# Two heads share one tile and one store in the last ten pairs of a decode block's backward pass

## The chip, the cores and the metric

The kernel runs on one core of one Trainium2 chip. The time is device microseconds of one execution of the whole program. The core has engines that run their own instruction streams in order: TensorE (PE, with its weight loads as PEld), VectorE (DVE), ScalarE (ACT), GpSimd (POOL) and SyncE (SP, which here only issues DMAs). DMAs run on 16 DMA engines that all queues share: q1 carries what SP issues, q0 what POOL issues, q10 what ScalarE issues.

## The reference, cut to what matters

The program is the forward pass of a transformer block for one new token, and the gradients of all its inputs. Two batches, 32 heads, a cache of 4096 rows of 128 numbers per head, everything in bfloat16:

```python
q = (x @ wq).reshape(B, Sq, Hq, Dh)                      # transposed to b h q d
scores = einsum("bhqd,bhkd->bhqk", q, k) * (Dh ** -0.5)
p = softmax(scores, axis=-1)
o = einsum("bhqk,bhkd->bhqd", p, v)                      # then @ wo
h  = x + attention(layernorm(x))
h2 = h + relu(layernorm(h) @ w1) @ w2
# outputs: h2 and the gradients of x, k_cache, v_cache, wq, wo, w1, w2
```

For one head with probabilities p (4096 numbers), query q, and go, the gradient of that head's attention output, the gradients of the caches are outer products: gV[s, :] = p[s] * go, and gK[s, :] = p[s] * (V[s, :] . go - o . go) * q * scale. Each is 1 MiB, and 64 heads (two batches) have both: 128 MiB are written for them alone, and 64 MiB of K and 64 MiB of V are read, most of V twice.

## The kernel before, in words

A head's 4096 rows lie on 128 partitions, 32 rows each (`NSC` = 32), so that a tile is [128, 32, 128] bfloat16: 8 KiB per partition, 1 MiB in all, one DMA (`load_tile`, L461). A first pass (`p1_iter`, L468) computes scores, softmax and the sums that the forward output needs, and keeps the probabilities in `P_bf`. Between the passes `middle_gen` (L746) and `go_group` (L683) make the MLP and the vectors `goc`, `gom`, `qsc`, `rt` and `negdot` of each head. A second pass takes the 64 heads in the order `turns`; some V tiles were kept, the other 52 are loaded again as `Wt`.

The second pass of one head is `p2_iter` (L869) and, one turn later, `p2_tail` (L848):

- PE spreads go and the scaled q of the head over 128 partitions into a PSUM bank `dp_ps` (L878); ScalarE copies that to `rb`, scaled by `rt` (L883); POOL makes `pp`, the probabilities, each written twice (L885).
- In four groups of eight row blocks, `pair_transpose` (L434) transposes V on PE (L442, two banks in turn), ScalarE copies the result to `t_sb` (L447), and `pair_matvec` (L450) multiplies it by go into `dp_ps` (L455).
- VectorE makes gV in two halves (`outer_half`, L841, at L843), and POOL stores it (L911). In the last three heads ScalarE makes four of the 32 row blocks of gV (L910, with `pf` from POOL).
- In the tail VectorE makes `gsp` = (dp + negdot) * p (L854), then gK in two halves (L843), and POOL stores it (L862).

The turn of head j runs the tail of head j - 1 between its own steps. All instructions are written out in this order by the program; nothing is rescheduled later. Between two steps of a turn, background generators put in one piece each: `fin_gen` (weight gradients, stored from `ot` on ScalarE's queue, L981), the rest of `middle_gen`, and `gx_gen`, whose 40 products over wq on VectorE (L669, `gxp`) fall into the last part of the run.

Large tiles come from one set of 8 KiB homes, which are lent under tags: `ld` for loads, `g` for gV and gK, `f` for `ot`, `q` for wq and w2 tiles. `share` says how many homes each tag may own at a stage. When the last go is known (j = 44), the memory of wo becomes free and gives six more homes: one `ld`, two `g`, three `q`; from then on `g` may own seven, `ld` six. A tile is free again when its store has landed. `pump` (L1149) issues the queue of loads in order as long as an `ld` home is free.

```python
for tag in ("ld", "g", "g", "q", "q", "q"):
    more_home(tag, big3)
...
share(ld=5 + held + more, g=5 + 2 * more, f=3, q=2 + 3 * more)
```

Of the kernel before, what the change touches and what calls it, by code (L numbers as in the profile page):

```python
# [7 lines left out]
FP32 = mybir.dt.float32  # L8
BF16 = mybir.dt.bfloat16
# [6 lines left out]
def kernel(  # L16
# [20 lines left out]
    nc = tc.nc  # L37
# [41 lines left out]


    NBIG = 13
    homes = {"ld": list(range(NBIG)), "g": [], "f": [], "q": []}
    free = {tag: len(v) for tag, v in homes.items()}
    owned = dict(free)
    wanted = {}
# [11 lines left out]

    def goes_to(tag):

        if owned[tag] > wanted.get(tag, len(pools)):  # L100
            for other in homes:
                if owned[other] < wanted.get(other, 0):
                    return other
        return tag
# [329 lines left out]
    def pair_transpose(nat, g, dve=False, busy=0):  # L434
# [12 lines left out]
            nc.scalar.copy(out=t_sb[:], in_=t_ps[:])  # L447
        return t_sb

    def pair_matvec(dst, t_sb, g, vecs):  # L450
        v = t_sb[:].bitcast(BF16).rearrange("p j (k two) -> p j k two", two=2)
        for j in range(GT // 2):
            sc = g * GT + 2 * j
            for par in range(2):
                nc.tensor.matmul(dst[:, sc:sc + 2], lhsT=v[:, j, :, par], rhs=vecs[:, par, :],  # L455
                                 start=(par == 0), stop=(par == 1))
# [4 lines left out]
    def load_tile(what, i, tag):  # L461
        t = take(tag, [128, NSC, 128], what + "t")
        nc.sync.dma_start(out=t[:], in_=natural(A_k_cache if what == "K" else A_v_cache,
                                                *(turns if what == "W" else pairs)[i]))
        (S2 if what == "W" else S1).setdefault(i, {})[what] = t
        (S2 if what == "W" else S1)[i][what + "g"] = tag

    def p1_iter(i, dve_group, busy):  # L468

# [378 lines left out]
    def p2_tail(j):  # L848

        p = S2[j]  # L850
        bp, hp = turns[j]
        pair_matvec(p["dp"], p.pop("T3"), 3, gom[:, bp, hp, :, :])
        gsp = small.tile([128, NSC, 2], BF16, tag="gsp", bufs=2, name="gsp")
        nc.vector.scalar_tensor_tensor(  # L854
            out=gsp[:], in0=p["dp"][:, :, None].to_broadcast([128, NSC, 2]), scalar=negdot[:, hp, bp:bp + 1],
            in1=P_bf[:, p_slot[(bp, hp)], :, None].to_broadcast([128, NSC, 2]), op0=ALU.add, op1=ALU.mult)
        yield
        gK = take("g", [128, NSC, 128], "gK")
        outer_half(gK, p["rb"][:, 128:256], gsp, 0)
        yield  # L860
        outer_half(gK, p["rb"][:, 128:256], gsp, 1)
        nc.gpsimd.dma_start(out=natural(out_2, bp, hp), in_=gK[:])  # L862
        give(gK)
        del S2[j]
        yield

    NSB = 8

    def p2_iter(j, nsb):  # L869

        tail = p2_tail(j - 1) if j - 1 in S2 and "T3" in S2[j - 1] else iter(())
# [12 lines left out]
        pp = small.tile([128, NSC, 2], BF16, tag="pp", bufs=2, name="pp")  # L884
        nc.gpsimd.tensor_copy(out=pp[:], in_=P_bf[:, p_slot[(b, h)], :, None].to_broadcast([128, NSC, 2]))  # L885
# [12 lines left out]
        c["T2"] = pair_transpose(c["W"], 2)  # L898
        pair_matvec(c["dp"], c.pop("T1"), 1, go)
        yield  # L900
        c["T3"] = pair_transpose(c["W"], 3)
        give(c["W"], "g" if j < H and j != 1 and owned["g"] < 3 else None)
        pair_matvec(c["dp"], c.pop("T2"), 2, go)
        gV = take("g", [128, NSC, 128], "gV")
        outer_half(gV, c["rb"][:, 0:128], c["pp"], 0)
        yield
        outer_half(gV, c["rb"][:, 0:128], c["pp"], 1, HALF - nsb)
        if nsb:
            for k in range(nsb):
                nc.scalar.activation(out=gV[:, NSC - nsb + k, :], in_=rb[:, 0:128], func=ACT.Copy, scale=pf[:, k:k + 1])  # L910
        nc.gpsimd.dma_start(out=natural(out_3, b, h), in_=gV[:])  # L911
        give(gV)
        yield
# [209 lines left out]
    while i <= NP1 + 1 or j <= NP1:  # L1123
        ii = i if i <= NP1 + 1 else None
        jj = j if i >= NP1 or (i >= P2_AT and (i - P2_AT) % 2 == 0) else None
        plan.append((ii, jj))
        i += 1
        if jj is not None:
            j += 1


    queue = []
# [3 lines left out]
    for n, (ii, jj) in enumerate(plan):  # L1136
        if ii is not None:
            if ii < NP1:
                queue.append(("K", ii))
        if ii is not None and ii >= 2:  # L1140
            queue.append(("V", ii - 2))
        ahead = plan[n + 1][1] if n + 1 < len(plan) and ii is not None else jj
        if ahead is not None and ahead < NP1 and turns[ahead] not in kept and ("W", ahead) not in queue:
            queue.append(("W", ahead))
        if ii in W_AT:
            queue.append(("w", W_AT.index(ii)))
        if ii in W2_AT:
            queue.append(("w2", W2_AT.index(ii)))
    def pump():  # L1149
        while queue:  # L1150
            what, k = queue[0]
            if what == "w":
                load_weights(k)
            else:
                tag = "ld"
                if free["ld"] < 1:
                    return
                if what == "w2":
# [24 lines left out]
    for n, (i, j) in enumerate(plan):  # L1183
# [7 lines left out]
        if all_go and not late[0]:  # L1191
            wop.release()
            big3 = tc.alloc_tile_pool(name="big3", bufs=1, side="right")
            for tag in ("ld", "g", "g", "q", "q", "q"):
                more_home(tag, big3)
        late[0] = all_go
        more = int(late[0])
        if fin is not None and not bg2 and not bg3:
            share(ld=8 + 3 * more, g=7 + 3 * more)
        elif fin is not None and j >= H:  # L1200
            held = sum(bh in kept for bh in turns[j + 1:])
            share(ld=5 + held + more, g=5 + 2 * more, f=3, q=2 + 3 * more)
        while g2 is not None:
            p2_step()
        open_tail = [k for k in S2 if "T3" in S2[k]]
        if j is not None:
            if j < NP1:
                bg_until(("go", *turns[j]))
            nsb = 0 if i is not None else NSB if j < H and fin is None else NSB // 2 if j >= NP1 - 3 else 0
            g2 = p2_iter(j, nsb) if j < NP1 else p2_tail(NP1 - 1)  # L1210
        elif open_tail:
            g2 = p2_tail(open_tail[0])
        if i is None and ("w1", 1) in done and fin is None:
# [17 lines left out]
        if i is None:  # L1231
            spread[0] = 2
            at_k[0] = 1
            k = 0
            while g2 is not None:
                p2_step()
                pump()
                slot[0] = int(k in ((1, 3, 5) if j <= H else (1, 4)))
# [69 lines left out]
```

## Time and profile before

| what | value |
|---|---|
| median of 3 runs | 894.2 us (891.58 to 896.1) |
| the profiled execution | 892.4 us |
| its span | 890.6 us |
| PE / VectorE / ScalarE / POOL busy | 83% / 77% / 53% / 23% |
| moved by DMA | 361.84 MB, mean 406 GB/s |
| q1 / q0 / q10, share of 16 engines | 58.1% / 36.2% / 4.1% |
| gV and gK stores | 64 each, 1024 KB, 15.1 and 15.4 us to landing |
| Wt loads | 52, 1024 KB, 11.8 us to landing |
| first gV store of the last 20 heads | issued at 705.65 us |

The busy shares are means over stages with different limits, so the stage of a change has to be looked at by itself. The page's slices give the tenths in which each engine is busy and the GB/s that the DMA engines moved; a DMA share of 1 means that all 16 engines had a packet all the time. Waits name what came last before an engine went on. "Packet records" are the DMA engines' own list of packets in the trace, with queue, size, start and duration of each; they do not say which of the 16 engines carried one.

### The profile page before, as it was taken

How to read it: one execution, taken by the hardware profiler on the slowest of the kernel's cores; microseconds unless marked ns; L12 is line 12 of the kernel's file. 1: busy time of each engine (PE TensorE's matmuls, PEld its weight loads, DVE VectorE, ACT ScalarE, POOL GpSimd, SP SyncE). 2: the span in 40 equal slices, each digit the busy share in tenths (PEclk: the TensorE clock that was granted, in tenths of full speed). 3: DMA queues.
4: the chain of work that ended last, by engine and by line, in shares of the span. 5: the costliest groups of instructions: out<-in, count | busy, mean ns of one | idle time of the engine just before them, and what ended most of it. 6: DMA issues, size and time to landing. Idle time of an engine off the chain costs nothing. (4 is left out here: it accounts for less than half of the span.)

```text
span 890.6 us, 24645 instructions
## 1 busy us (share of the span) xinstructions
PE 740.5 (83%) x10145; PEld 622.4 (70%) x10145; DVE 687.8 (77%) x1283; ACT 469.7 (53%) x1184; POOL 204.3 (23%) x342
## 2 busy tenths in 40 slices
PE   4999899999999998888888767885888888658871
PEld 4887788888887887777777656764666665536561
DVE  2665779876789897796796888786988467899992
ACT  1344334443455665454547766554567766437751
POOL 1344434342310000000023321121323011111141
PEclk9999989999999999997995555555557765555555
DMA  9999999999889999999999999999999999999995
GB/s 377 419 411 404 409 407 419 410 415 408 350 325 369 422 422 424 422 421 424 422 390 423 420 419 420 419 416 416 391 404 413 424 425 425 424 426 424 423 421 245
DMA packets 56304, 361.84 MB, mean 406 GB/s; under 512 B 5696, under 2 KB 11904, under 8 KB 15488
## 3 DMA queue, kind: packets, MB, share of 16 engines
q1 hardware_dynamic: 34536, 211.13, 58.1%
q0 software_dynamic: 18432, 134.23, 36.2%
q10 hardware_dynamic: 3224, 14.92, 4.1%
q8 instruction: 80, 1.31, 0.6%
q14 instruction: 32, 0.26, 0.1%
HBM read 211.11 MB, written 149.13 MB: 404 GB/s over the span
## 5 line engine op out<-in xcount | busy, mean ns | idle before, releaser
L447 ACT COPY t_sb<-t_ps 128x512 f32<-128x512 f32 x479 | 273.1, 587 | 186.3 <-PE t_ps L442 181.7
L455 PEld LDWEIGHTS <-t_sb 128*128 128x128 bf16 x4096 | 169.9, 103 | 83.7 <-ACT t_sb L447 42.3
L442 PE MATMUL t_ps<-ident_f,Wt 128*128 128x128 f32 x832 | 201.0, 393 | 0.4 <-ACT t_sb L447 0.4
L483 DVE TENSOR_TENSOR pk<-Kt,ep 128x2048 bf16<-128x2048 bf16 x128 | 156.2, 1221 | 44.7 <-ACT ep L534 24.9
L476 PE MATMUL m_ps<-pk,Vt 128*128 128x129 bf16 x2048 | 176.1, 223 | 13.3 <-DMA Vt<-in_A_v_cache_dram 12.6
L843 DVE TENSOR_TENSOR gK<-rb,gsp 128x2048 bf16<-128x2048 bf16 x128 | 153.8, 1226 | 28.0 <-DMA out_dram<-gV 26.2
L843 DVE TENSOR_TENSOR gV<-rb,pp 128x2048 bf16<-128x2048 bf16 (+2 forms) x128 | 147.1, 1172 | 30.8 <-DMA out_dram<-gK 24.0
L442 PEld LDWEIGHTS t_ps<-ident_f,Wt 128*128 128x128 f32 x832 | 140.4, 205 | 31.9 <-issue 25.0
L442 PE MATMUL t_ps<-ident_f,Kt 128*128 128x128 f32 x1024 | 154.7, 287 | 4.6 <-DMA Kt<-in_A_k_cache_dram 4.5
L476 PEld LDWEIGHTS <-Vt 128*128 128x128 bf16 x2048 | 131.0, 99 | 16.9 <-DMA Vt<-in_A_v_cache_dram 14.9
L442 PEld LDWEIGHTS t_ps<-ident_f,Kt 128*128 128x128 f32 x1024 | 117.0, 148 | 6.1 <-issue 3.4
L493 POOL COPY pk<-ep 128x16 bf16<-128x16 bf16 x80 | 83.1, 1041 | 151.3 <-ACT ep L534 112.7
L455 PE MATMUL dp_ps<-gom,t_sb 128*128 128x2 bf16 x2048 | 96.0, 168 | 23.3 <-ACT t_sb L447 22.9
L911 POOL DMA_DIRECT2D out_dram<-gV x64 | 34.3, 536 | 307.8 <-DVE nb L526 114.3
L455 PE MATMUL s_ps<-gom,t_sb 128*128 128x2 bf16 x2048 | 80.2, 164 | 1.2 <-DVE t_sb L445 1.2
L862 POOL DMA_DIRECT2D out_dram<-gK x64 | 34.1, 533 | 202.0 <-DVE gK L843 156.8
L593 ACT CAST MT<-m_ps 128x128 bf16<-128x128 f32 x64 | 17.1, 266 | 116.3 <-PE m_ps L476 116.3
L978 ACT CAST ot<-o_ps 128x512 bf16<-128x512 f32 (+3 forms) x152 | 67.0, 498 | 9.7 <-DMA out_dram<-ot 8.5
L883 ACT ACTIVATE rb<-dp_ps,rt 128x256 bf16<-128x256 f32 x64 | 30.2, 472 | 46.5 <-PE dp_ps L878 44.8
L669 DVE CUSTOM_DVE_ANT_0 rows<-wo_t,rows 128x640 bf16<-128x640 bf16 x64 | 52.3, 817 | 0.4 <-ACT rows L647 0.2
L669 DVE CUSTOM_DVE_ANT_0 rows<-wqs,gqr 128x1024 bf16<-128x1024 bf16 x40 | 48.8, 1219 | 0.2
L669 DVE CUSTOM_DVE_ANT_0 rows<-w_t,rows 128x640 bf16<-128x640 bf16 (+2 forms) x58 | 45.8, 790 | 1.2 <-ACT rows L647 0.5
(194 smaller groups left out, 720.4 us busy)
## 6 DMA issues: line engine op xcount, KB each, us to landing
Kt<-in_A_k_cache_dram SPq DMA_DIRECT2D x64, 1024.0 KB, 16.4
Vt<-in_A_v_cache_dram SPq DMA_DIRECT2D x64, 1024.0 KB, 16.6
out_dram<-gV POOLq DMA_DIRECT2D x64, 1024.0 KB, 15.1
out_dram<-gK POOLq DMA_DIRECT2D x64, 1024.0 KB, 15.4
Wt<-in_A_v_cache_dram SPq DMA_DIRECT2D x52, 1024.0 KB, 11.8
out_dram<-ot ACTq DMA_DIRECT2D x6, 960.0 KB, 12.4
wq_t<-in_A_wq_dram SPq DMA_DIRECT2D x5, 1024.0 KB, 11.0
wqs<-in_A_wq_dram SPq DMA_DIRECT2D x5, 1024.0 KB, 16.1
```

Source lines behind the costliest of these rows:

```text
L442: nc.tensor.transpose(t_ps[:, j, :], natf[:, 2 * cc:2 * cc + 2, :].rearrange("p c k -> p (c k)"), ident_f[:])
L447: nc.scalar.copy(out=t_sb[:], in_=t_ps[:])
L455: nc.tensor.matmul(dst[:, sc:sc + 2], lhsT=v[:, j, :, par], rhs=vecs[:, par, :], start=(par == 0), stop=(par == 1))
L476: nc.tensor.matmul(r["m"][:, 0:129], lhsT=r["V"][:, sc, :], rhs=r["pk"][sc // HALF][:, sc % HALF, 0:129], start=(sc == 0), stop=(sc == NSC ...
L483: nc.vector.tensor_tensor(out=p["pk"][k][:, :, 0:128].rearrange("p s (a two) -> p s a two", two=2), in0=p["K"][:, sl, :].rearrange("p s (a ...
L493: nc.gpsimd.tensor_copy(out=col, in_=e)
L669: nc.vector.tensor_tensor_reduce(out=junk[0:kc, 0:width], in0=in0, in1=in1, scale=1.0, scalar=0.0, op0=ALU.mult, op1=ALU.add, accum_out=acc)
L843: nc.vector.tensor_tensor(out=pairs_view(dst[:, sl, :]), in0=row.rearrange("p (a two) -> p a two", two=2)[:, None, :, :].to_broadcast([128 ...
L862: nc.gpsimd.dma_start(out=natural(out_2, bp, hp), in_=gK[:])
L883: nc.scalar.activation(out=rb[:], in_=bank[:, 128:384], func=ACT.Copy, scale=rt[:, b, h:h + 1])
L911: nc.gpsimd.dma_start(out=natural(out_3, b, h), in_=gV[:])
L978: nc.scalar.copy(out=ot[0:P, k, n0:n0 + nn], in_=o_ps[0:P, 0:nn])
```

## The change

The last 20 heads of the second pass (j from 44 on, `PAIRS_AT`) are made two by two. Partitions 0 to 63 hold the first head and 64 to 127 the second, so that a partition has 64 rows of one head instead of 32. Two loads of 1 MiB bring V of the pair: each takes 32 of the 64 rows of every partition. `rb`, `pp`, `gsp` are built by halves of the partitions: PE spreads the vectors over 64 partitions each, the probabilities are brought to their partitions by matmuls with `sel` and copied from PSUM by ScalarE, POOL copies the two values of `rt` to one column, and `gsp` is two VectorE instructions of 64 partitions. There are eight groups of transposes and matvecs per pair, whose matvecs serve both heads. gV and gK of a pair are tiles of 16 KiB per partition, made in four `outer_half` instructions each and stored by one DMA of 2 MiB, 16 KiB contiguous per partition; the last pair's two tiles are stored in two halves each. The memory of wo becomes three homes of 16 KiB (`gp`) instead of six of 8 KiB, and the other homes that held gV and gK go to the loads. ScalarE no longer makes part of gV in the last heads.

```diff
-    homes = {"ld": list(range(NBIG)), "g": [], "f": [], "q": []}
+    homes = {"ld": list(range(NBIG)), "g": [], "f": [], "q": [], "gp": []}
...
+    def both_matvec(dst, t_sb, g, vecs):
+        v = t_sb[:].bitcast(BF16).rearrange("p j (k two) -> p j k two", two=2)
+        for j in range(GT // 2):
+            sc = g * GT + 2 * j
+            for par in range(2):
+                nc.tensor.matmul(dst[:, :, sc:sc + 2], lhsT=v[:, j, :, par], rhs=vecs[:, :, par, :],
+                                 start=(par == 0), stop=(par == 1))
...
+    def pair_natural(cache, b, h):
+        return cache[b, h:h + 2].rearrange("h (p sc) d -> (h p) sc d", sc=2 * NSC)
+
+    def load_half(i, k, tag):
+        t = take(tag, [128, NSC, 128], "Wt")
+        nc.sync.dma_start(out=t[:], in_=pair_natural(A_v_cache, *turns[i])[:, k * NSC:(k + 1) * NSC, :])
+        S2.setdefault(i, {})[f"W{k}"] = t
...
+    def by_half(dst, src, h):
+        for k in range(2):
+            rows = slice(64 * k, 64 * k + 64)
+            nc.gpsimd.tensor_copy(out=dst[rows], in_=src[rows, h + k:h + k + 1])
+
+    def both_tail(j):
+        p = S2[j]
+        bp, hp = turns[j]
+        both_matvec(p["dp"], p.pop("T7"), 7, gom[:, bp, hp:hp + 2, :, :])
+        gsp = spare(2)
+        for k in range(2):
+            rows = slice(64 * k, 64 * k + 64)
+            nc.vector.scalar_tensor_tensor(
+                out=gsp[rows], in0=p["dp"][rows, k, :, None].to_broadcast([64, 2 * NSC, 2]),
+                scalar=negdot[rows, hp + k, bp:bp + 1], in1=p["pp"][rows], op0=ALU.add, op1=ALU.mult)
+        yield
+        gK = take("gp", [128, 2 * NSC, 128], "gK")
+        dst = pair_natural(out_2, bp, hp)
+        for k in range(4):
+            outer_half(gK, p["rb"][:, 128:256], gsp, k)
...
+            nc.gpsimd.dma_start(out=dst, in_=gK[:])
...
+    def both_iter(j):
...
+        for k, col in enumerate((goc, qsc)):
+            for q in range(2):
+                nc.tensor.matmul(bank[64 * q:64 * q + 64, 128 + k * 128:256 + k * 128],
+                                 lhsT=col[:, h + q, b:b + 1].to_broadcast([128, 64]), rhs=ident_bf[:],
+                                 start=True, stop=True)
+        pps = bank[:, 384:512].rearrange("p (k q s) -> p k q s", k=2, q=2)
+        for q in range(2):
+            for k in range(2):
+                nc.tensor.matmul(pps[:, k, q, :], lhsT=sel[:, q, :, :].rearrange("p c k -> p (c k)"),
+                                 rhs=P_bf[:, p_slot[(b, h + k)], :], start=True, stop=True)
...
+        by_half(rts, rt[:, b, :], h)
+        rb = mats.tile([128, 256], BF16, tag="rb", bufs=3, name="rb")
+        nc.scalar.activation(out=rb[:], in_=bank[:, 128:384], func=ACT.Copy, scale=rts)
+        pp = spare(j // 2 % 2)
+        for k in range(2):
+            rows = slice(64 * k, 64 * k + 64)
+            nc.scalar.copy(out=pp[rows].rearrange("p (q s) t -> p q s t", q=2),
+                           in_=pps[rows, k, :, :, None].to_broadcast([64, 2, NSC, 2]))
...
+        for g in range(1, 8):
+            W = c[f"W{g // 4}"]
+            c[f"T{g}"] = pair_transpose(W, g % 4)
...
+            both_matvec(c["dp"], c.pop(f"T{g - 1}"), g - 1, go)
+            if g >= 4:
+                if gV is None:
+                    gV = take("gp", [128, 2 * NSC, 128], "gV")
+                outer_half(gV, c["rb"][:, 0:128], c["pp"], g - 4)
...
+            nc.gpsimd.dma_start(out=pair_natural(out_3, b, h), in_=gV[:])
...
+    PAIRS_AT = 2 * H - 2 * (H - 2 * KEPT[1]) // 2
...
-            for tag in ("ld", "g", "g", "q", "q", "q"):
-                more_home(tag, big3)
+            for _ in range(3):
+                more_home("gp", big3)
...
-            share(ld=8 + 3 * more, g=7 + 3 * more)
+            share(ld=16)
...
-            share(ld=5 + held + more, g=5 + 2 * more, f=3, q=2 + 3 * more)
+            share(ld=5 + held + 3 * more, g=5 if not more else int(j == PAIRS_AT), f=3, q=2 + 3 * more)
...
-            g2 = p2_iter(j, nsb) if j < NP1 else p2_tail(NP1 - 1)
+            g2 = both_iter(j) if PAIRS_AT <= j < NP1 else p2_iter(j, nsb) if j < NP1 else both_tail(NP1 - 2)
```

More of the change, by code (lines that the diff above doesn't have):

```diff
@@ L98, in goes_to @@
     def goes_to(tag):
-        if owned[tag] > wanted.get(tag, len(pools)):
+        if tag != "gp" and owned[tag] > wanted.get(tag, len(pools)):
             for other in homes:
@@ L865, in p2_tail, with tail_of, spare @@
         yield
+    def tail_of(j):
+        if j - 1 in S2 and "T3" in S2[j - 1]:
+            return p2_tail(j - 1)
+        if j - 2 in S2 and "T7" in S2[j - 2]:
+            return both_tail(j - 2)
+        return iter(())
+    def spare(k):
+        return P_bf[:, 2 + 4 * k:6 + 4 * k, :].rearrange("p a (s t) -> p (a s) t", t=2)
+    def by_half(dst, src, h):
+        for k in range(2):
+            rows = slice(64 * k, 64 * k + 64)
+            nc.gpsimd.tensor_copy(out=dst[rows], in_=src[rows, h + k:h + k + 1])
@@ new lines, in both_tail @@
+    def both_tail(j):
[13 more added lines that the diff above has]
+            outer_half(gK, p["rb"][:, 128:256], gsp, k)
+            if j == NP1 - 2 and k == 1:
+                nc.gpsimd.dma_start(out=dst[:, 0:NSC, :], in_=gK[:, 0:NSC, :])
+            if k < 3:
+                yield
+        if j == NP1 - 2:
+            nc.gpsimd.dma_start(out=dst[:, NSC:2 * NSC, :], in_=gK[:, NSC:2 * NSC, :])
+        else:
+            nc.gpsimd.dma_start(out=dst, in_=gK[:])
+        give(gK)
+        del S2[j]
+        yield
@@ new lines, in both_iter @@
+    def both_iter(j):
+        tail = tail_of(j)
+        c = S2[j]
+        next(tail, None)
+        b, h = turns[j]
+        go = gom[:, b, h:h + 2, :, :]
+        bank = pst([128, 512], FP32, "sps", "dp_ps")
+        for k, col in enumerate((goc, qsc)):
[8 more added lines that the diff above has]
+                                 rhs=P_bf[:, p_slot[(b, h + k)], :], start=True, stop=True)
+        c["dp"] = bank[:, 0:4 * NSC].rearrange("p (k s) -> p k s", k=2)
+        rts = Uc[:, 0, j // 2 % 2:j // 2 % 2 + 1]
+        by_half(rts, rt[:, b, :], h)
[6 more added lines that the diff above has]
+                           in_=pps[rows, k, :, :, None].to_broadcast([64, 2, NSC, 2]))
+        c.update(rb=rb, pp=pp)
+        c["T0"] = pair_transpose(c["W0"], 0)
+        next(tail, None)
+        yield
+        for _ in tail:
+            yield
+        gV = None
+        for g in range(1, 8):
+            W = c[f"W{g // 4}"]
+            c[f"T{g}"] = pair_transpose(W, g % 4)
+            if g % 4 == 3:
+                give(W)
+            both_matvec(c["dp"], c.pop(f"T{g - 1}"), g - 1, go)
[3 more added lines that the diff above has]
+                outer_half(gV, c["rb"][:, 0:128], c["pp"], g - 4)
+                if j == NP1 - 2 and g == 5:
+                    nc.gpsimd.dma_start(out=pair_natural(out_3, b, h)[:, 0:NSC, :], in_=gV[:, 0:NSC, :])
+            yield
+        if j == NP1 - 2:
+            nc.gpsimd.dma_start(out=pair_natural(out_3, b, h)[:, NSC:2 * NSC, :], in_=gV[:, NSC:2 * NSC, :])
+        else:
+            nc.gpsimd.dma_start(out=pair_natural(out_3, b, h), in_=gV[:])
+        give(gV)
+        yield
+        yield
@@ L867 @@
     NSB = 8
+    PAIRS_AT = 2 * H - 2 * (H - 2 * KEPT[1]) // 2
     def p2_iter(j, nsb):
-        tail = p2_tail(j - 1) if j - 1 in S2 and "T3" in S2[j - 1] else iter(())
+        tail = tail_of(j)
         c = S2[j]
@@ L1128 @@
         if jj is not None:
-            j += 1
+            j += 2 if PAIRS_AT <= jj < NP1 else 1
     queue = []
@@ L1143 @@
         if ahead is not None and ahead < NP1 and turns[ahead] not in kept and ("W", ahead) not in queue:
-            queue.append(("W", ahead))
+            queue += [("X", (ahead, 0)), ("X", (ahead, 1))] if ahead >= PAIRS_AT else [("W", ahead)]
         if ii in W_AT:
@@ L1157, in pump @@
                     return
-                if what == "w2":
+                if what == "X":
+                    load_half(*k, tag)
+                elif what == "w2":
                     w2_tiles[k] = load_w2(k, tag)
@@ L1193 @@
             big3 = tc.alloc_tile_pool(name="big3", bufs=1, side="right")
-            for tag in ("ld", "g", "g", "q", "q", "q"):
-                more_home(tag, big3)
+            for _ in range(3):
+                more_home("gp", big3)
+            assert j == PAIRS_AT
         late[0] = all_go
@@ L1208 @@
                 bg_until(("go", *turns[j]))
+                assert j < PAIRS_AT or ("go", *turns[j + 1]) in done
             nsb = 0 if i is not None else NSB if j < H and fin is None else NSB // 2 if j >= NP1 - 3 else 0
-            g2 = p2_iter(j, nsb) if j < NP1 else p2_tail(NP1 - 1)
+            g2 = both_iter(j) if PAIRS_AT <= j < NP1 else p2_iter(j, nsb) if j < NP1 else both_tail(NP1 - 2)
         elif open_tail:
@@ L1237 @@
                 pump()
-                slot[0] = int(k in ((1, 3, 5) if j <= H else (1, 4)))
+                slot[0] = int((k if j < PAIRS_AT else k % 7) in ((1, 3, 5) if j <= H else (1, 4)))
                 k += 1
```

## The prediction, made before the run

> **What bounds the kernel now.** I read the page's slices first, then the stretches of the last stage, then the DMA engines alone at the very end, then the instructions there, and last the groups and waits of the stage that the change touches (from about 700 us on).
>
> The page, 40 slices of 22.3 us:
>
> ```profile
> DMA  9999999999889999999999999999999999999995
> GB/s 377 419 411 404 409 407 419 410 415 408 350 325 369 422 422 424 422 421 424 422 390 423 420 419 420 419 416 416 391 404 413 424 425 425 424 426 424 423 421 245
> DMA packets 56304, 361.84 MB, mean 406 GB/s; under 512 B 5696, under 2 KB 11904, under 8 KB 15488
> ```
>
> From slice 31 on the 16 DMA engines move 421 to 426 GB/s without a break: the stage is bound by the bytes and by what each packet costs. Stretches of the end, with PE, PEld, DVE, ACT and POOL busy, then granted clock, DMA share and GB/s:
>
> ```profile
> 820.00:840.00 20.00, 17.20 (x140) 10.01 (x138) 18.68 (x27) 15.66 (x33) 2.94 (x6) 0.66 1.02 424
> 840.00:850.00 10.00, 7.83 (x75) 6.47 (x74) 9.97 (x13) 5.85 (x11) 1.47 (x3) 0.50 1.01 423
> 850.00:860.00 10.00, 7.08 (x75) 6.45 (x76) 9.73 (x21) 3.40 (x6) 4.22 (x6) 0.50 1.01 422
> 860.00:870.00 10.00, 9.30 (x85) 7.72 (x84) 9.93 (x16) 7.01 (x17) 5.93 (x9) 0.50 1.00 416
> 870.00:880.00 10.00, 1.08 (x19) 0.85 (x17) 4.58 (x6) 1.81 (x6) 1.67 (x4) 0.50 1.01 418
> 880.00:891.00 11.00, 0.00 (x0) 0.00 (x0) 0.00 (x0) 0.00 (x0) 0.00 (x0) 0.50 0.13 57
> ```
>
> VectorE is a near second: 9.7 to 10.0 of every 10 us between 840 and 870. The end itself, DMA alone (40 slots of 0.275 us from 880 to 891):
>
> ```profile
> GB/s 447 328 298 179 149 89 89 60 60 30 30 30 0 30 30 30 30 30 30 30 30 30 0 30 30 30 30 30 30 30 0 0 0 0 0 0 0 0 0 0
> q0 software_dynamic: 96, 0.62, 13.5%
> ```
>
> Fifteen engines are done by about 882.5; 30 GB/s is one engine alone, and it works until 888.5, without a gap. That engine's queue is the end of the kernel. The last instructions:
>
> ```profile
> 872.25 2.36 DVE L843 TENSOR_TENSOR gK<-rb,gsp 128x2048 bf16<-128x2048 bf16 x2
> 872.67 0.53 POOL L911 DMA_DIRECT2D out_dram<-gV  x1 [1.81 <-ACT gV L910]
> 874.91 0.53 POOL L862 DMA_DIRECT2D out_dram<-gK  x1 [1.71 <-DVE gK L843]
> ```
>
> The last store is issued at 874.9. In the packet records a store puts eight packets on each engine, 305.8 ns apart, 2.45 us in all, so on the late engine its turn is 886.0 to 888.5: compute ends 11.1 us before its data is wanted. That lead is what the change can spend. The stage's groups and VectorE's waits for store tiles:
>
> ```profile
> L843 DVE TENSOR_TENSOR gK<-rb,gsp 128x2048 bf16<-128x2048 bf16 x40 | 47.9, 1226 | 12.9 <-DMA out_dram<-gV 12.5
> L843 DVE TENSOR_TENSOR gV<-rb,pp 128x2048 bf16<-128x2048 bf16 x37 | 44.3, 1219 | 13.5 <-DMA out_dram<-gK 9.7 <-ACT ot L978 3.5 <-ACT GQr L938 0.3
> L669 DVE CUSTOM_DVE_ANT_0 rows<-wqs,gqr 128x1024 bf16<-128x1024 bf16 x40 | 48.8, 1219 | 0.2
> L885 POOL COPY pp<-P_bf 128x64 bf16<-128x64 bf16 x19 | 8.8, 465 | 0.0
> ```
>
> ```profile
> DVE gK L843 <- DMA out_dram<-gV: 12.5, 7, 4.6
> DVE gV L843 <- DMA out_dram<-gK: 9.7, 5, 3.0
> ```
>
> The profiled execution took 892.4 us (span 890.6 and 1.8 around it), 1.8 below the median of 894.2. Changes are worked out against it and then added to the median.
>
> **The change, part by part.**
>
> *Packets.* Bytes stay. Of the 40 stores of 1 MiB, 36 become 18 of 2 MiB with 16 KiB rows; the last pair is still stored in four halves of 8 KiB rows. In the packet records of this stage 4096 B take 159 ns and 8192 B 309 ns (these for reads and writes alike); each starts 3 ns before the one ahead ends. A straight line leaves some 6 ns per packet that is not bytes. Each engine loses 144 packets and 18 completion writes of about 6 ns: 0.9 + 0.1 = 1.0 us on the late engine, the one place where something comes off the path. Above it stand the only 16 KiB packets in the trace, instruction loads, with 940 ns here where the line gives 609: 144 x 0.33 = 48 us. I take the line, since 8 KiB instruction loads lie on it (309) and stores are nearer to stores; the other end is a rival.
>
> *Loads.* Twenty V loads of 1 MiB stay twenty, in nearly the old order on SP's queue (one instead of two behind the last wq load). They now read 8 KiB out of every 16. Nearest row: the grad-wq stores write 4 KiB out of every 8, at the 159 ns of the line. So nothing; the other end is under the rivals. [...]
>
> *VectorE.* 80 outer products stay 80 at 1.22 us. The 20 gsp (0.278 us, 128x64) become 20 of 64x128; reductions from PSUM of 32 and 128 columns take 0.188 and 0.289, so 64 columns more are 0.067 each, 1.3 us in all (bounds 0 and, by a 64x64 copy of 0.50, 4.4). ScalarE's help with gV in the last three heads goes: 3 x (1.219 - 0.944) = 0.8 us back to VectorE.
>
> *ScalarE, POOL, PE.* ScalarE drops ten rb (0.47) and twelve column products (0.39) and gets twenty 64-row copies (nearest cast 128x128, 0.28): 9.4 us out, 5.6 in. POOL loses 18 issues of 0.53, all pp and pf copies, and gets twenty copies of one column (0.25 to 1.3 by its copies of few elements). PE gets 40 matmuls of 32 columns at 0.17, 0.7 us a pair. All this lies beside a VectorE that is fuller, except for one new wait: rb now needs POOL's small copies, which stand behind the store of the pair before, which waits for its fourth gV product. Behind rb on ScalarE stand the pair's PSUM copies, and PE waits for those banks. From that fourth product to the pair's last matvec: issue 0.53, two copies 0.5 to 2.6, rb 0.47, two copies 0.56, then eight groups. The last head's four groups took 5.4 us (866.2 to 871.6) and four more are 1.14 apart: 10.0, less 1.9 for the two groups whose transposes are done meanwhile. The chain is 10.2 to 12.3, middle 11.2. VectorE's own pair is 8 x 1.22 + 0.7 = 10.4. Each gsp waits for the chain, so a pair takes half of 11.2 + 10.4, 10.8 us, against 9.65 for two heads now (gV stores at 863.02 and 872.67).
>
> *Tiles.* Seven 1 MiB store tiles become three of 2 MiB. Two queued tiles last the late engine 9.8 us; filling the third takes 4.9 and an issue, so the queue does not run dry by itself. But VectorE may be at least 1 MiB less ahead, and half a tile more on average: 2.45 to 4.9 us, I take 3.7. More tiles go to loads instead.
>
> *The sum.* Spent from the lead of 11.1: three pairs without products of wq between (L669), 3 x (10.8 - 9.65) = 3.5 (2.3 to 5.0; ScalarE's lost help is in it); the longer gsp of the seven pairs before, 14 x 0.067 = 0.9 (0 to 3.1); the smaller queue 3.7 (2.5 to 4.9); issue to first packet 1 (0.5 to 2). Together 9.1, so 2 us of cover are left and nothing of it reaches the end. At the upper ends it is 15.0, and 3.9 come out. Net -1.0, at worst here +2.9. Time: 892.4 - 1.0 = 891.4, against the median 894.2 - 1.0 = **893.2 us**, own range 891.5 to 897.
>
> **Rivals.**
>
> *Three tiles are too few (slower).* Between the last load (about 830) and the last wq product (851), a fill carries two wq products of 1.30 as well: 4.9 + 2.6 + 0.35 + 0.53 and the landing's way back, 8.4 to 10, against 9.8 us of queued stores. Past 9.8 the late engine runs dry at every fill. One us too much at four fills, on top of the 3.9 above: +8 - 1 = +7, **901 us**. For it: VectorE at 9.7 to 10.0 of 10. Against it: a 16 KiB packet takes more of each turn beside 8 KiB loads, so more stores may be out before the loads end.
>
> *Large packets or half rows are slow (slower).* If stores take the 940 ns, or half-row loads twice 309, the stage grows by 48 or 49 us: **943 us**; a tenth of that is already 899.
>
> *The late engine is less late (faster).* Its 6 us behind the other fifteen decide the end. If fewer, larger stores leave the engines more even, up to 6 us go: 894.2 - 1 - 6 = **887 us**. For it: no work of its own explains the lag. Against it: every store and load gives each engine the same eight rows, before and after.
>
> **How the numbers follow.** A measurement here can tell about 0.5% (889.7 to 898.7) from no change. The likeliest case has 0.58, and all of it lies inside. Too few tiles: 0.25, of which 0.06 stays below 898.7. Slow packets or rows: 0.07. Less late engine: 0.10. So faster 0.10, same 0.64, slower 0.26. The range leaves out the slow packets, half of the less-late-engine case and the worst of too few tiles: 889 to 902.
>
> **What would show it.** Right: 2304 data packets fewer at the same 361.84 MB; DMA share 1.01 up to about 880; 16 KiB packets of about 609 ns; a last store issued only some 2 us before its turn on the late engine; gsp waiting about a microsecond for PE in the last pairs. Wrong: DMA below 400 GB/s in a stretch between 820 and 875 while VectorE is full (too few tiles), VectorE waiting long for gV or gK landings with the DMA full but GB/s lower (slow packets), or an end at which no single engine is left (the lag gone).

## The result, and the profile after

The changed kernel takes 903.3 us (median of 6 runs, 903.15 to 908.05) against 893.8 us for the kernel before on the same chip: a ratio of 1.0119, 95% interval 1.0094 to 1.0145. The change makes the program about 10 us slower. The profiled execution took 903.15 us, its span is 901.4 us, 10.8 more than before.

The page of the changed kernel, the rows of the DMA engines in 40 slices of 22.5 us:

```profile
DMA  9999999999989999999999999999999989999886
GB/s 376 419 410 405 409 406 420 410 414 407 343 344 373 421 424 423 421 424 423 415 399 425 420 417 416 422 416 413 389 419 413 404 319 425 425 424 424 372 347 279
DMA packets 53712, 361.84 MB, mean 401 GB/s; under 512 B 5408, under 2 KB 11616, under 8 KB 15200
```

The bytes are the same in 2592 packets fewer. Two places differ in the last stage: slice 33 (319 GB/s, 721 to 744 us), and the last three slices, where before only the last one was low. The stretches of the end of the changed kernel, with PE, PEld, DVE, ACT and POOL busy, granted clock, DMA share and GB/s:

```profile
820.00:840.00 20.00, 16.31 (x160) 11.15 (x158) 16.00 (x21) 14.28 (x31) 0.56 (x2) 0.67 1.02 427
840.00:850.00 10.00, 5.99 (x32) 3.00 (x31) 9.83 (x15) 5.35 (x12) 2.56 (x4) 0.50 0.85 349
850.00:860.00 10.00, 10.00 (x80) 6.88 (x80) 9.97 (x13) 7.42 (x15) 1.69 (x3) 0.50 0.87 359
860.00:870.00 10.00, 9.52 (x91) 8.70 (x90) 9.66 (x21) 5.11 (x11) 0.89 (x2) 0.51 0.80 327
870.00:880.00 10.00, 5.60 (x70) 4.73 (x69) 8.74 (x12) 3.71 (x8) 3.27 (x4) 0.66 0.88 367
880.00:890.00 10.00, 4.66 (x55) 4.11 (x53) 8.32 (x10) 2.35 (x4) 1.59 (x3) 0.50 0.92 379
```

From 840 to 870 VectorE is full (9.7 to 10.0 of every 10 us, then 8.7 and 8.3) and the DMA engines are not: 327 to 379 GB/s where the kernel before kept 416 to 424 up to 880. The loads are through (the last V load is issued at 820), and what is left is stores that VectorE has yet to make. The last instructions, and one from the beginning of the pairs, from the timeline:

```profile
719.90 2.36 DVE L859 TENSOR_TENSOR gK<-rb,gsp 128x2048 bf16<-128x2048 bf16 x2 [25.64 <-DMA out_dram<-gV]
...
885.99 4.63 DVE L859 TENSOR_TENSOR gK<-rb,P_bf 128x2048 bf16<-128x2048 bf16 x4
888.64 0.53 POOL L916 DMA_DIRECT2D out_dram<-gK  x1 [3.41 <-DVE gK L859]
890.91 0.53 POOL L920 DMA_DIRECT2D out_dram<-gK  x1 [1.74 <-DVE gK L859]
```

The last store is issued at 890.91, 16.0 us later than before. Its last packet ends at 895.7 by the packet records, 4.8 us after the issue instead of 13.6: so 8.8 of the 16.0 were hidden, and the DMA engines end 7.2 us later. (The 4.8 are more than one store's own 2.45 because the store issued at 888.64 is still moving when the last one is issued.) The other 3.6 us lie behind the last packet: the span ends 5.7 us after it, before 2.1. Together 10.8.

In these lines `P_bf` stands for `pp` and `gsp` of a pair, which lie in its memory: L907 makes gsp. Groups of the stage from 700 us on (busy, mean ns of one, then idle time before them), and VectorE's and one of ScalarE's waits there (total, times, longest):

```profile
L685 DVE CUSTOM_DVE_ANT_0 rows<-wqs,gqr 128x1024 bf16<-128x1024 bf16 x40 | 48.8, 1220 | 0.4
L859 DVE TENSOR_TENSOR gV<-rb,P_bf 128x2048 bf16<-128x2048 bf16 x40 | 47.3, 1218 | 0.0
L859 DVE TENSOR_TENSOR gK<-rb,P_bf 128x2048 bf16<-128x2048 bf16 x40 | 46.9, 1220 | 0.3
L897 POOL COPY Uc<-rt 64x1 f32<-64x1 f32 x18 | 14.2, 790 | 0.9
L907 DVE SCALAR_TENSOR_TENSOR P_bf<-dp_ps,negdot,P_bf 64x128 bf16<-64x128 f32 x20 | 7.0, 348 | 9.4 <-PE dp_ps L455 9.0
```

```profile
DVE gK L859 <- DMA out_dram<-gV: 25.6, 1, 25.6
DVE P_bf L907 <- PE dp_ps L455: 9.0, 4, 4.1
DVE ml L752 <- PE mlp_ps L748: 6.9, 1, 6.9
DVE rows L679 <- PE row_ps L676: 2.3, 2, 2.0
ACT rb L949 <- POOL Uc L897: 31.8, 5, 17.2
```

The products cost what they cost before. All waits for store tiles but one are gone; that one lasts 25.6 us. In their place VectorE waits for PE, and ScalarE's rb waits for POOL's small copies. The 25.6 us are the most visible line of the profile, and the first theory was that they are the loss.

### The profile page after: what moved, and what is told of

It reads as the page before. It is cut to its first block, busy times and chain, and to the rows that moved or that the text cites. A ratio compares the mean times of both kernels' runs of the same rounds, so it can differ in the third digit from the quotient of the medians.

```text
span 901.4 us, 24663 instructions
## 1 busy us (share of the span) xinstructions
PE 740.7 (82%) x10185; PEld 622.3 (69%) x10185; DVE 690.5 (77%) x1283; ACT 466.4 (52%) x1182; POOL 196.4 (22%) x321
## 5 line engine op out<-in xcount | busy, mean ns | idle before, releaser
L463 PEld LDWEIGHTS <-t_sb 128*128 128x128 bf16 x3456 | 138.4, 101 | 65.8 <-ACT t_sb L447 33.0
L442 PEld LDWEIGHTS t_ps<-ident_f,Wt 128*128 128x128 f32 x832 | 139.3, 203 | 28.2 <-issue 23.8
L442 PE MATMUL t_ps<-ident_f,Kt 128*128 128x128 f32 x1024 | 152.7, 285 | 4.4 <-DMA Kt<-in_A_k_cache_dram 4.4
L492 PEld LDWEIGHTS <-Vt 128*128 128x128 bf16 x2048 | 130.7, 99 | 17.2 <-DMA Vt<-in_A_v_cache_dram 15.3
L859 DVE TENSOR_TENSOR gK<-rb,gsp 128x2048 bf16<-128x2048 bf16 x88 | 105.8, 1227 | 38.1 <-DMA out_dram<-gV 36.1
L859 DVE TENSOR_TENSOR gV<-rb,pp 128x2048 bf16<-128x2048 bf16 x88 | 100.2, 1159 | 20.7 <-DMA out_dram<-gK 13.4
L463 PE MATMUL dp_ps<-gom,t_sb 128*128 128x2 bf16 x1408 | 65.5, 168 | 17.2 <-ACT t_sb L447 16.9
L1028 POOL DMA_DIRECT2D out_dram<-gV x44 | 23.5, 535 | 234.4 <-DVE nb L542 113.8
L1095 ACT CAST ot<-o_ps 128x512 bf16<-128x512 f32 (+3 forms) x152 | 66.8, 493 | 10.2 <-DMA out_dram<-ot 7.2
L878 POOL DMA_DIRECT2D out_dram<-gK x44 | 23.4, 532 | 157.2 <-DVE gK L859 127.1
L859 DVE TENSOR_TENSOR gV<-rb,P_bf 128x2048 bf16<-128x2048 bf16 x40 | 47.3, 1218 | 0.0
L859 DVE TENSOR_TENSOR gK<-rb,P_bf 128x2048 bf16<-128x2048 bf16 x40 | 46.9, 1220 | 0.3
## 6 DMA issues: line engine op xcount, KB each, us to landing
Vt<-in_A_v_cache_dram SPq DMA_DIRECT2D x64, 1024.0 KB, 18.2
out_dram<-gV POOLq DMA_DIRECT2D x9, 2048.0 KB, 12.8
```

Of the source, the lines that this page charges most:

```text
L442: nc.tensor.transpose(t_ps[:, j, :], natf[:, 2 * cc:2 * cc + 2, :].rearrange("p c k -> p (c k)"), ident_f[:])
L492: nc.tensor.matmul(r["m"][:, 0:129], lhsT=r["V"][:, sc, :], rhs=r["pk"][sc // HALF][:, sc % HALF, 0:129], start=(sc == 0), stop=(sc == NSC ...
L859: nc.vector.tensor_tensor(out=pairs_view(dst[:, sl, :]), in0=row.rearrange("p (a two) -> p a two", two=2)[:, None, :, :].to_broadcast([128 ...
L1095: nc.scalar.copy(out=ot[0:P, k, n0:n0 + nn], in_=o_ps[0:P, 0:nn])
```

## Theory A: the stall at the hand-over

At j = 44, `share` hands the 8 KiB homes of `g` away from the front of the list, oldest first, and leaves one for gK of head 43. What is left is the newest, the one that gV of head 43 has just given back: gK of head 43 must wait until that store (issued at 694.36) has crossed a full queue. Theory A: these 25.6 us, less the 3.5 that the same instruction waited before, put VectorE behind for the rest of the run. Theory B: the pairs themselves are slow.

One run gives gK the oldest home instead, with every engine's instructions in the same order (e1); the other does the opposite to the kernel before (e2):

```diff
+            if j == PAIRS_AT:
+                homes["g"].append(homes["g"].pop(0))
             share(ld=5 + held + 3 * more, ...)
```

```diff
...
             share(ld=5 + held + more, ...)
+            if j == 2 * H - 20:
+                homes["g"].remove(last_g[0])
+                homes["g"].insert(0, last_g[0])
```

> The changed kernel with one thing else: when the homes are shared out at j = 44, the home that stays with gK of head 43 is the one given back first (its store landed long ago) instead of the one that gV of head 43 gave back last. Every engine's instructions and their order stay. Theory A, the hand-over stalls VectorE: gK of head 43 no longer waits 25.6 us but under 4; VectorE's 22 us come back, the DMA engines are full from 690 to about 880 again, and the time falls from 903 to 893, range 889 to 897. Rival B, the pairs themselves are slow (three tiles of 2 MiB, rb behind the store of the pair before): the wait goes, or moves to another tile, the time stays at 900 to 904, and the windows from 840 on stay below 390 GB/s. In between, 897 to 900, both have a share.

> The kernel before, with one thing else: at j = 44 the home that gV of head 43 has just given back comes first in the list, so that gK of head 43 must wait for that store, as in the changed kernel; nothing else of the change is in it. Theory A: one wait of about 25 us at that gK; the 7 tiles of 1 MiB that are free behind it cannot be filled in that time, the DMA engines run out of stores for some 5 us between 710 and 745 (as the share of 0.76 in 720 to 740 shows for the changed kernel), and the time rises by 4 to 10, to 898 to 904. Rival B, the stall is harmless because VectorE has slack of 18 us of waits for tiles behind it: 893 to 896, with those waits gone instead.

Measured: e1 904.4 us, ratio to before 1.0135 (1.0114 to 1.0155); e2 893.8 us, 1.0025 (1.0007 to 1.0042). VectorE's waits between 690 and 890 us in e1, and then in e2:

```profile
DVE P_bf L907 <- PE dp_ps L455: 17.8, 3, 11.6
DVE rows L685 <- DMA wqs<-in_A_wq_dram: 12.8, 2, 6.5
DVE gV L859 <- DMA out_dram<-gK: 4.7, 2, 2.6
DVE ml L752 <- PE mlp_ps L748: 4.4, 1, 4.4
DVE gK L859 <- DMA out_dram<-gV: 3.4, 1, 3.4
```

```profile
DVE gK L846 <- DMA out_dram<-gV: 23.4, 3, 21.0
DVE gsp L857 <- PE dp_ps L458: 7.0, 4, 2.9
DVE gV L846 <- DMA out_dram<-gK: 1.7, 1, 1.7
```

Theory A fell from both sides. Without the long wait the changed kernel is no faster, since other waits (for PE, for tiles of wq) take its place; with it the kernel before loses about a quarter of a percent (0.07 to 0.42), since it makes up for most of it with tiles that have come free meanwhile (its waits for tiles fall from 28.2 us in all to 25.1, of which 21.0 are the stall). A wait that is long and alone is not yet a cost: what counts is what the engine could have done in that time.

## What VectorE is late for

Two runs measured VectorE itself. e5 takes some 12 us of products over wq away from the changed kernel, e6 adds 15.2 us of them to the kernel before:

```diff
-                    ttr(t[:, k * GW:(k + 1) * GW], ..., GW, junk=junk)
+                    n = 64 if c >= 2 and b == 1 else GW
+                    ttr(t[:, k * GW:k * GW + n], ..., n, junk=junk)
```

```diff
+                    for _ in range(2 if c >= 2 and b == 1 else 1):
                         ttr(t[:, k * GW:(k + 1) * GW], ..., GW, junk=junk)
```

> The changed kernel with less work on VectorE in its last part: 12 of the 40 products over wq (those of the second batch from the third tile on) read 64 of their 1024 columns, so this part of the gradient of x is left out; loads, stores, tiles and the order of everything stay. That takes some 12 us (12 x about 1.05) from VectorE between about 775 and 870. Theory C, after 760 VectorE is the bound of the changed kernel, and every us that it is behind at 760 comes out at the end: the time falls by 8 to 12, to 891 to 895, where the DMA engines are the bound again. Rival D, the three tiles or the waits for PE set the pace: VectorE only waits longer, and the time stays above 899.

> The kernel before with more work on VectorE: the same 12 products over wq are made twice, 12 x 1.27 = 15.2 us more between about 770 and 865, with nothing else changed. It measures the lead: the last store is issued 11.1 us before its turn at the late DMA engine, and VectorE still waits for tiles for some 8 us after 740, which more work can fill. By the lead as the prediction took it, 0 to 11 us are hidden and the time rises by 4, range 0 to 7 (893 to 900). If VectorE has no lead that can be spent, it rises by 12 to 15, to 905 to 908.

Measured: e5 900.9 us, 1.0079 (1.0056 to 1.0102); e6 898.6 us, 1.0053 (1.0036 to 1.0069). In e6 the last store is issued 11.2 us later and the last packet ends 3.9 us later: of 15.2 us, 4.0 went into waits that VectorE had anyway and 7.3 were hidden behind the last store. In e5 the last store comes only 5.4 us earlier than in the changed kernel, for 12 us less work; the time is 0.40%, 3.6 us, lower, with intervals that overlap. VectorE's waits after 760 us in the changed kernel, and then in e5:

```profile
DVE P_bf L907 <- PE dp_ps L455: 6.9, 3, 4.1
DVE rows L679 <- PE row_ps L676: 2.3, 2, 2.0
```

```profile
DVE P_bf L907 <- PE dp_ps L455: 11.4, 4, 4.5
DVE rows L685 <- DMA wqs<-in_A_wq_dram: 3.5, 1, 3.5
DVE rows L679 <- PE row_ps L676: 2.3, 2, 2.0
```

So neither theory of e5 was right alone: VectorE sets the pace after 760, but PE's half of a pair and the tiles of wq are right behind it: its waits grow from 9.2 to 17.2 us, which takes back 8 of the 12. The cause had to be looked for in what VectorE waits on. Four single edits on e1 did that.

**e3, POOL's copies one pair ahead.** In the changed kernel the two copies of `rt` (L897) stand on POOL behind the store of the pair before, and rb waits for them.

```diff
-        by_half(rts, rt[:, b, :], h)
+        if j == PAIRS_AT:
+            by_half(rts, rt[:, b, :], h)
...
+        if j + 2 < NP1:
...
+            by_half(Uc[:, 0, nk_:nk_ + 1], rt[:, nb_, :], nh_)
```

> As the run with the oldest home, and POOL's two copies of rt for the next pair are issued one pair ahead, in front of the store of gV instead of behind it. So rb no longer waits for that store. Theory: gsp's waits for PE, 9.0 us in four, shrink to under 2 us in all; if VectorE is what the last pairs are bound by, the time is 1 to 4 us below that of the run with the oldest home. Rival, the DMA engines are the bound again once the stall is gone: within 1 us of that run.

Measured 900.7 us, 1.0099 (1.0070 to 1.0128), 3.7 us below e1 on the same chip; the intervals of the two overlap, and in the traces the last store is issued 4.0 us earlier and the span is 3.0 us shorter. rb's waits for POOL fell from 27.7 us to 4.3. gsp still waits 16.5 us for PE, most of it (10.2) in the first pair, so the part of the expectation on gsp was wrong.

**e8, six homes for loads instead of eight.** The only change is the number in `share`.

```diff
-            share(ld=5 + held + 3 * more, ...)
+            share(ld=5 + held + more, ...)
```

> As the run with the oldest home, but the loads own six homes in the last stage, as in the kernel before, instead of eight; two homes lie idle. If the two extra homes let loads run ahead of stores and of the wq tiles (VectorE waits for these 12.8 us in that run, 6.5 before its first product over wq), these waits shrink, stores get a larger share earlier, and the time falls by 3 to 6 against 904.4. If the loads only come when PE frees a home anyway, it stays within 1.5 us, or rises where PE now waits for V tiles.

Measured 900.5 us, 1.0068 (1.0047 to 1.0089). With six homes other homes are left over at j = 44, and gK of head 43 waits 18.2 us again; the time falls all the same, and the last store is issued 4.2 us earlier. SyncE's issues, in e1 and then in e8:

```profile
691.55 20.68 SPq L481 DMA_DIRECT2D Wt<-in_A_v_cache_dram  x5
718.69 0.33 SPq L379 DMA_DIRECT2D w_t<-in_B_w_dram  x1
723.63 2.95 SPq L1142 DMA_DIRECT2D wqs<-in_A_wq_dram  x2
```

```profile
694.83 15.22 SPq L481 DMA_DIRECT2D Wt<-in_A_v_cache_dram  x3
710.41 0.33 SPq L379 DMA_DIRECT2D w_t<-in_B_w_dram  x1
710.98 23.54 SPq L1142 DMA_DIRECT2D wqs<-in_A_wq_dram  x2
```

SyncE issues in order. With eight homes five V loads go ahead of the first tiles of wq, with six three do, and the first tile of wq is asked for 12.7 us earlier. VectorE's waits for wq tiles, 12.8 us in e1, are gone in e8, and in 820 to 840, 840 to 850 and 850 to 860 the DMA engines move 420, 433 and 419 GB/s (e1: 395, 326 and 341). That the number of homes costs 4 to 6 us is shown; that the order on SyncE's queue is how, is read from the two traces and was not tested by itself. In the changed kernel itself VectorE waits for no wq tile, so there the cost can only be read from the time: e8, which has a wait at the hand-over too, is 0.51% below it.

**e4, stores in halves.** The pairs remain, each tile is stored in two halves of 8 KiB rows, as the last pair's are.

```diff
-            if j == NP1 - 2 and k == 1:
+            if k == 1:
...
-        if j == NP1 - 2:
+        if True:
```

> As the run with the oldest home, and every gV and gK of a pair is stored as the last pair's are: in two halves of 1 MiB with 8 KiB rows, each issued when its two products are made. So the pairs remain and the single store of 16 KiB rows goes. Theory, a packet costs 6 ns beside its bytes and the earlier issue only fills a queue that isn't empty: 1 us slower than that run, range 0 to +2. Rival, the larger tile makes the data late (the first half waits 2.4 us for the second): 1 to 4 us faster than that run, with more GB/s from 840 on.

Measured 899.4 us, 1.0079 (1.0057 to 1.0101), 5.0 us below e1: the theory had the wrong sign. The rival's reason does not hold either. In the trace the last store comes later than in e1 (893.3 against 890.4), and so does the last packet (897.7 against 896.2). What is shorter is the time behind the last packet. SyncE's waits at the end of the kernel before, of the changed one and of e4; by the records what ends at that time, before all engines meet, is the drain that POOL begins behind its last store (at 889.9, 900.6 and 899.0):

```profile
SPq L1303 <- PEq L1303: 1.0, 2, 0.5
```

```profile
SPq L1424 <- PEq L1424: 4.6, 2, 4.1
```

```profile
SPq L1426 <- PEq L1426: 1.0, 2, 0.5
```

The two profiled executions differ by 2.2 us (903.75 and 901.57): 3.6 less in the drain, 1.5 more up to the last packet. The other 2.8 us of the 5.0 between the medians no trace shows, since the profiled execution of e4 is the slowest of its four.

**e7, gsp earlier.** The last matvec of a pair and its gsp are put one step after its last transposes, ahead of two pieces of background work.

```diff
...
         give(gV)
         yield
+        c["tail"] = both_tail(j)
+        next(c["tail"])
         yield
...
```

> As the run with the oldest home, and the last matvec of a pair and its gsp are issued one step after the last group of transposes, not three steps later behind two pieces of background work. If what puts VectorE behind at 760 is that gsp of a pair stands behind eight groups and the background pieces between them on PE (waits for PE of 11.6, 2.1 and 4.1 us in that run), these waits fall to about half and the time falls by 3 to 6 against 904.4. If the place is taken by other waits (tiles, wq tiles), it stays within 1.5 us.

Measured 902.6 us, 1.0101 (1.0069 to 1.0134): alone it is not told from e1. gsp's waits for PE fell from 17.8 to 13.7 us, and a wait for PE's MLP product grew from 4.4 to 8.6.

## Putting the edits together

> Three edits at once on the run with the oldest home: six homes for loads instead of eight, POOL's copies of rt one pair ahead, and every pair's gV and gK stored in two halves. Alone they gave 900.5, 900.7 and 899.4 against 904.4, so 3.9, 3.7 and 5.0 us. If these are three separate costs, they add up and the time is 892 (890 to 895), level with the kernel before: then the change's loss is these three. If they are one cost seen three ways (VectorE behind by the same us each time), the time stays near the best of them, 897 to 900.

> Two of these edits, six homes for loads and the early copies, with the single 2 MiB stores of the changed kernel kept. In all six traces with 2 MiB stores POOL's last instruction, a drain, ends 4.9 to 5.4 us after the last packet, in all four without them 1.3 to 1.4. If that is what the halves gain, this run is 3.5 us above the run with three edits, and its drain again ends about 4.9 us after the last packet. If the halves gain by making data ready earlier, the difference is also there in the time of the last packet.

> The changed kernel, with the stores of its last three pairs in two halves each instead of those of the last pair alone; fourteen stores of 2 MiB remain, the last of them some 40 us before the end. It asks what makes the drain long. If a drain only waits for large stores that are still in work, its end goes back to 1.35 us after the last packet and the time falls by about 3.5, to 900. If 2 MiB stores anywhere in the program make it long, it stays at 4.9 us and the time within 1.5 us of 903.3.

> The run with three edits, and besides the last matvec and gsp of a pair one step after its last transposes. Alone that gave 902.6 against 904.4, which the runs don't tell from nothing. If waits of gsp for PE still hold VectorE up once the other three costs are gone, 1 to 3 us below the run with three edits; if the DMA engines are the bound again, within 1 us.

> As the run with four edits, and at j = 44 the two homes left for gV and gK are taken oldest first. In that run gK of head 43 still waits 23.5 us for the store of gV of head 43 (six homes for loads leave other homes over than eight do), and the DMA engines are idle for 0.21 x 10 + 0.02 x 20 = 2.5 us between 710 and 740. If that stall counts once the other costs are gone, the wait goes and the time falls by 1 to 3, to 891 to 893, level with the kernel before or just below it. If it is as harmless as in the run with the oldest home and in the kernel before, within 1 us of 893.9.

> As the run with five edits, and ScalarE makes 8 of the 64 row blocks of gV in the last two pairs, as it makes 4 of 32 in the last three heads of the kernel before. That takes 2 x 0.6 us from VectorE behind the last product over wq. If VectorE still sets the end of the last two pairs (the DMA share is 0.79 and 0.96 in 860 to 880), the time falls by about 1 us; if PE's groups do, it stays, or rises by up to 1 us since ScalarE also copies what PE transposes.

The edits are those above (e9: e3, e8 and e4 together; e12: e3 and e8; e11: e9 and e7). e10 changes the condition of the halves from `j == NP1 - 2` to `j >= NP1 - 6` in the changed kernel. e13 and e14 add:

```diff
             share(ld=5 + held + more, ...)
+            if j == PAIRS_AT:
+                homes["g"].sort(key=given_at.get)
```

```diff
...
+                nsb = NSB if pf is not None and g == 7 else 0
+                outer_half(gV, c["rb"][:, 0:128], c["pp"], g - 4, HALF - nsb)
+                for k in range(nsb):
+                    nc.scalar.activation(out=gV[:, 2 * NSC - nsb + k, :], ..., scale=pf[:, k:k + 1])
```

All runs, with the end of each profiled execution (the last two columns from the records of POOL's instructions and of the packets):

| run | median us | ratio to before, 95% | last store issued | last packet ends | drain ends after it |
|---|---|---|---|---|---|
| before | 892.4 to 893.8 | 1 | 874.9 | 888.5 | 1.4 |
| after | 903.3 | 1.0119 (1.0094 to 1.0145) | 890.9 | 895.7 | 4.9 |
| e1 oldest home | 904.4 | 1.0135 (1.0114 to 1.0155) | 890.4 | 896.2 | 4.9 |
| e2 before, newest home | 893.8 | 1.0025 (1.0007 to 1.0042) | 875.2 | 888.5 | 1.4 |
| e3 early copies | 900.7 | 1.0099 (1.0070 to 1.0128) | 886.4 | 893.3 | 4.9 |
| e4 halves | 899.4 | 1.0079 (1.0057 to 1.0101) | 893.3 | 897.7 | 1.3 |
| e5 less on VectorE | 900.9 | 1.0079 (1.0056 to 1.0102) | 885.5 | 891.3 | 4.9 |
| e6 before, more on VectorE | 898.6 | 1.0053 (1.0036 to 1.0069) | 886.1 | 892.4 | 1.3 |
| e7 early gsp | 902.6 | 1.0101 (1.0069 to 1.0134) | 890.0 | 894.9 | 4.9 |
| e8 six homes | 900.5 | 1.0068 (1.0047 to 1.0089) | 886.2 | 890.4 | 5.4 |
| e10 last three pairs in halves | 900.0 | 1.0081 (1.0056 to 1.0106) | 892.6 | 896.4 | 0.8 |
| e12 = e3 + e8 | 897.2 | 1.0050 (1.0033 to 1.0066) | 884.3 | 891.4 | 4.9 |
| e9 = e12 + halves | 895.8 | 1.0039 (1.0026 to 1.0053) | 885.2 | 890.4 | 1.4 |
| e11 = e9 + early gsp | 893.9 | 1.0012 (1.0000 to 1.0025) | 886.7 | 892.1 | 1.3 |
| e13 = e11 + old homes first | 892.7 | 1.0000 (0.9990 to 1.0011) | 881.3 | 888.9 | 1.4 |
| e14 = e13 + ScalarE's share | 892.4 | 1.0000 (0.9987 to 1.0012) | 881.2 | 888.4 | 1.4 |

- The costs are partly separate: e9 was expected at 892 if they added up and at 897 or more if they were one; it took 895.8. In ratio, the three edits bring 0.96% of e1's 1.35% back; their single gains add up to 1.59%.
- The drain: 4.9 to 5.4 us after the last packet in all seven traces with 2 MiB stores near the end, 0.8 to 1.4 in all nine without. e10 keeps fourteen such stores, none in the last three pairs, and has 0.8; its time fell 3.4 us, as expected, though its interval overlaps that of the changed kernel; the spans of the two traces differ by 3.5. Between e12 and e9 the spans differ by 4.5 us, but the medians by 1.4 only, with overlapping intervals: the 3.5 us show in one trace of each and the times do not tell them.
- The early gsp gives 1.9 us once the rest is gone (e11 against e9 on one chip, intervals apart). The profiled executions of the two lie the other way round, so the traces do not show where; it rests on the medians of 12 runs each.
- The stall at the hand-over: e13 takes it out of e11, gains 1.2 us and has its last store 5.4 us earlier. The intervals of e11 and e13 overlap, so whether that is the stall's is not told; more than some 3 us it isn't.
- ScalarE's share of gV in the last two pairs gives nothing that these runs can tell.

e13 has pairs of heads, three tiles of 16 KiB per partition and all the matmuls and copies of the change, and takes the time of the kernel before. What it no longer has is the single store of 2 MiB: its stores are halves of 8 KiB rows. In its stretches the DMA engines have fewer holes:

```profile
840.00:850.00 10.00, 10.00 (x72) 7.26 (x72) 9.97 (x12) 6.91 (x14) 1.06 (x2) 0.50 1.01 423
850.00:860.00 10.00, 7.70 (x84) 6.30 (x83) 9.80 (x19) 5.27 (x11) 1.65 (x5) 0.67 0.93 384
860.00:870.00 10.00, 7.55 (x92) 6.65 (x91) 9.79 (x17) 4.41 (x10) 2.03 (x4) 0.67 0.87 356
870.00:880.00 10.00, 4.51 (x60) 3.77 (x57) 9.95 (x13) 2.90 (x5) 2.13 (x4) 0.67 0.99 400
```

No version was clearly faster than the kernel before.

## Why the prediction was wrong, point by point

The step that failed is the spending of VectorE's lead. The sum had VectorE's last store 9.1 us later, all of it hidden; it came 16.0 us later. The term with no price, "More tiles go to loads instead", costs 4 to 6 us, the new wait of rb was too small, and POOL's drain, 3.5 us, was not in the sum.

- *What bounds the kernel, and the lead of 11.1 us.* The kind is right, the size a little large. 15.2 us more on VectorE (e6) cost the kernel before 0.53%, 4.7 us (3.2 to 6.2), but 4.0 of them filled waits. Behind the last store 7.3 us were hidden in e6 and 8.8 in the changed kernel, where the prediction had 11.1 less 1 for the issue.
- *Packets.* Right in what it counted: 2592 records fewer, 2304 of them data and 288 completions, and a 16 KiB packet of a store takes 611 ns in the median of the packet records (the line gave 609). The gain of 1.0 us can't be seen, because in the changed kernel the DMA engines stand idle for more than that before the end.
- *Loads.* Right. Packets of the half-row loads take 309 ns in the median, as whole rows do. The "twice 309" and the 49 us of the rival are shown by no run.
- *VectorE.* Right: the twenty gsp took 7.0 us instead of 5.6, 1.4 more (1.3 predicted), and the products the same. ScalarE's lost help was put at 0.8 us; e14 shows no gain from giving it back.
- *ScalarE, POOL, PE, the new wait of rb.* The mechanism was right, the size and the place were not. It was counted for the three pairs behind the last product of wq, with 3.5 us. It acts in the pairs before them too (rb waits 31.8 us for POOL, five times, part of it in the long stall), and taking it away (e3) gives 3 to 4 us by medians and traces with all other delays still in place, which the overlapping intervals of e1 and e3 don't confirm. The last pair takes 12.4 us, from the store of one gV at 872.31 to the second half of the next at 884.71, where the prediction had 10.8; with the edits of e13 it takes 10.3 (865.69 to 876.03).
- *Tiles.* The largest part of what failed. The smaller queue was given 3.7 us, and after 740 VectorE waits for no store tile at all. The sentence "More tiles go to loads instead" was given nothing, and it costs 3.9 us by the medians, 6.0 by the ratios (e8 against e1). It was taken for a gift, and is an order: whoever owns a home decides what SyncE's queue holds ahead of what.
- *The hand-over at j = 44.* Not in the prediction. The list of homes was not followed tile by tile; the wait of 25.6 us that it makes is the largest of the profile and cost little.
- *The sum.* 9.1 us of VectorE's lead were to be spent, 16.0 were; 8.8 of them were hidden, 7.2 came out. The records of VectorE say where: its last product over wq ends 10.2 us later than before (860.3 against 850.1), where the sum had 4.6 for the longer gsp and the smaller queue, and from there to the last store it takes 30.6 us instead of 24.8, 5.8 more, where the sum had 3.5. The edits part along this line too: with six homes (e8) the first time is 855.6 and the second stays 30.6, and with the early copies besides (e12) the second is 27.6. Another 3.5 lie in POOL's drain, which no term held and no row of the kernel before could show.
- *Rivals.* "Three tiles are too few" named 901 us, near the 903.3 by chance, and its sign came: below 400 GB/s between 820 and 875 with VectorE full. But VectorE never waits for a tile there, and e13 has the same three tiles at 892.7. A sign that fits two causes told nothing of which. "Large packets or half rows are slow" did not come. "The late engine is less late" is half seen: in the changed kernel the last engine ends 0.6 us behind the others instead of 6, but because all of them ran dry; in e13, where they are fuller again, one engine alone works for the last 2.5 us, at 30 GB/s.

## What to carry to other kernels

When memory changes owner, price the new owner as well as the old one: which queue may now run ahead, and what stands behind it there. The longest wait of a profile is a question, and both directions answer it cheaply: take it out of the slow kernel, and put it into the fast one. Measure the lead by adding work to the engine that is to spend it; here 7 to 9 us of the predicted 11 could be hidden, and small delays, most of them of its suppliers, spent 16.

## What had not been expected of the hardware

POOL's drain at the end of the program ends 4.9 to 5.4 us after the last packet when the pairs before the last one were stored as single DMAs of 2 MiB with 16 KiB per partition, even though the last four stores are of 1 MiB, and 0.8 to 1.4 us after it when the last three pairs or all of them are stored in halves. Why is open; the packets of the last store itself end 3.8 to 7.5 us after its issue in the changed kernel and its variants, in both groups.

One DMA engine ends behind the rest where stores are queued to the end: by 6 us in the kernel before, by 3.1 in e2 with the last packet at the same 888.5, by 2.5 in e13. The Trainium skill (DMA: Bandwidth & Descriptors, Latency and other measured facts) says that two of the sixteen engines are usually slower than the rest; the packet records here do not name the engine, so no run shows whether it is one of them.
